# Attention values taken for two or three blocks of queries in one group of matmuls

## The chip, the cores and the metric

The kernel runs on one core of one Trainium2 chip. The metric is the device time of one execution in microseconds (us). The engines are named as in the profile: PE is TensorE's matmul, PEld its weight load, DVE is VectorE, ACT is ScalarE, POOL is GpSimd and SP is SyncE, which only issues transfers here.

## What is computed

There are 8 batches of 8 heads, 576 positions of 64 numbers each, in fp32. The attention weights are thresholded before they are normalised, and its output, with the heads side by side, goes through a feed-forward layer of 4608 tokens, 512 to 2048 to 512, with a squared ReLU.

```python
scores = scale * np.matmul(q, k.transpose(0, 1, 3, 2))
thresh = np.max(scores, axis=-1, keepdims=True) - tau
scores = np.where(scores >= thresh, scores, -1000000000.0)
scores = scores - np.max(scores, axis=-1, keepdims=True)
attn = np.exp(scores)
attn = attn / (np.sum(attn, axis=-1, keepdims=True) + 1e-09)
attn_out = np.matmul(attn, v)
x = attn_out.transpose(0, 2, 1, 3).reshape(B * S, H * D)
h = x @ w_in
r = np.maximum(h, 0.0)
out = (r * r) @ w_out
```

## The kernel before

The heads are taken in pairs, 32 pairs in all. The 576 queries of a pair are four blocks of 128 and one of 64 (NBLK is 4, REST is 64). A visit is a pair with a list of blocks, and a step is one block of one visit. Visits 0 to 3 take blocks 0 and 1 of the first four pairs, visits 4 to 7 take blocks 2, 3 and 4 of the same pairs, and from visit 8 on a visit takes all five blocks. So visits 0 to 3 are steps 0 to 7, visits 4 to 7 are steps 8 to 19, and visits 8, 9 and 10 are steps 20 to 34. Below, "v1 b1" is block 1 of visit 1.

One step goes through these stations:

- *Scores* (`scores`, L273, or L266 for the block of 64): PE multiplies the queries by the 576 keys, for both heads, into four of the eight PSUM banks. The next step's scores use the same four banks.
- *Maxima* (L310), exponents (L325 on ACT) and *threshold* (L337 on DVE): the threshold reads the scores a last time, and after it the banks are free for the next step's scores.
- *Division* (`divide`, L347 on POOL): the weights are normalised.
- *Turning*: for the values the weights are wanted with the keys on the partitions. Up to visit 10, PE turns them: `turn` transposes a block in three parts (L386; L393 and L399 for the block of 64), each into a PSUM bank, and ACT copies each part into `wT` (L387, L395, L400). This happens two steps after the block's own step. From visit 11 on (`by_dma`), DVE and transfers turn the weights instead.
- *Values* (`mix`, L502): PE multiplies the values v by the turned weights. One head gives 64 columns of output and the two heads stand side by side. For one block there are 10 fp32 matmuls (5 groups of keys, two heads), each of them two records in the trace. ACT then puts the result into `xT` (`put`, L485), the input of the feed-forward layer.

Two of the PSUM banks (4 and 5) serve the turns and the values in turn (`take("tx", (4, 5))`). A value group or a turn that gets a bank waits until ACT has copied out what stood there.

For visits 0 to 10 the values of a block are taken three steps after its own step. The table `mixes` says in which step which columns are taken, and the loop at the end of the kernel reads it. In such a step the order on PE is: scores of the step, first two parts of the turn of the block two steps back, perhaps a piece of the feed-forward layer, the values of the block three steps back, the third part of the turn, and further pieces.

A *piece* is a small part of the feed-forward layer for 256 tokens (a chunk). Pieces fill PE's time beside attention: `rate(s)` says how many us of pieces a step should take, a quarter of it is offered in four places of the step (`fill`), and a piece counts as PIECE_US, 1.76 us. Up to step `out_from` (34) the rate spreads the pieces of chunk 0 evenly over the steps that are left. A piece of the first product (L548) or the second (L730) of chunk 0 also waits until enough of the weights have been rounded. The rounding of the feed-forward weights is 32 parts, from step 2 to 33, one in most steps and two in steps 15, 18 and 22; one part takes two operations on ACT (L149, L150), two on DVE (L152, L154) and two on POOL (L156, L158). Chunk 0 is there from step 10, when the values of visit 3 have been taken. From step 35 on the pieces of chunk 1 follow.

All engines are scheduled by hand: each runs its instructions in the order in which the kernel emits them.

Of the kernel before, what the change touches and what calls it, by code (L numbers as in the profile page):

```python
# [19 lines left out]
def kernel(  # L20
# [10 lines left out]
    nc = tc.nc  # L31
    B, H, S, D = q.shape
    d_model, d_ff = moe_w_in.shape
    n_tokens = out.shape[0]
    P = 128
    HP = H // 2
    NPAIR = B * HP
    NBLK = S // P
    REST = S - NBLK * P
# [37 lines left out]
    wT = const.tile([P, S // REST + 1, NC9, REST], FP32, name="wT")  # L77
# [3 lines left out]
    at = RAW * 2 * WP  # L81
# [16 lines left out]
    g = const.tile([P, NFT, TCH], FP32, name="g")  # L98
# [104 lines left out]
    def arrived(t):  # L203
        assert all(x[0].tensor.name != t.tensor.name for x in loads)
# [149 lines left out]
    def take(what, among):  # L354
        used[what] += 1
        return bank[among[used[what] % len(among)]]
# [15 lines left out]
    def keep_bank(what):  # L372
# [2 lines left out]
        kept[what] = used["bank"]  # L375
        return to

    def turn(vis, i, part):

        w = weights[vis, i][0]  # L380
        ps = take("mm", (6, 7)) if early() and part == 1 else take("tx", (4, 5))
        ps = ps.rearrange("p (c n) -> p c n", n=P)
        if i < NBLK:
            for n in range(3):
                c = 3 * part + n
                nc.tensor.transpose(ps[:, n, :], w.rearrange("p u k -> p (u k)")[:, c * P:(c + 1) * P], ident)  # L386
            nc.scalar.copy(wT[:, 2 * i:2 * i + 2, 3 * part:3 * part + 3, :].rearrange("p g c q -> p c g q"),  # L387
                           ps[:, 0:3, :].rearrange("p c (g q) -> p c g q", g=2))
        elif part < 2:
            rows = slice(part * D, (part + 1) * D)  # L390
            for c in range(NBLK):
                at = part * REST + c * P
                nc.tensor.transpose(ps[:, c, 0:D], w[rows, 0, at:at + P], ident[rows, rows])  # L393
            at = part * (NBLK + 1)
            nc.scalar.copy(wT[:, 2 * NBLK, at:at + NBLK, :], ps[:, :, 0:D])  # L395
        else:

            for rows, keys in ((slice(0, D), slice(S - REST, S)), (slice(D, P), slice(0, REST))):
                nc.tensor.matmul(ps[rows, 0, 0:D], w[rows, 0, keys], ident[rows, rows], start=True, stop=True)  # L399
            nc.scalar.copy(wT[:, 2 * NBLK, NBLK, :], ps[:, 0, 0:D])  # L400

    blocks = {}
    outside = {}
# [66 lines left out]
    def put(n, first, ps, by_32s):  # L470

        b, pr = divmod(visits[n][0], HP)
        count = ps.shape[1]
        lo = (b * S + first) % RING
        assert b * S + first + count - RING <= read_to["x"]

        def to(x0, x1):
            at = (lo + x0) % RING
            return xT[:, pr, at:at + x1 - x0]

        fit = min(RING - lo, count)
        if not by_32s:
            for x0, x1 in ((0, fit), (fit, count)):
                if x0 < x1:
                    nc.scalar.copy(to(x0, x1), ps[:, x0:x1])  # L485
            return
        src = ps.rearrange("p (b u q) -> p b u q", u=2, b=4)
        if fit == count:
            nc.scalar.copy(to(0, count).rearrange("p (u b q) -> p b u q", u=2, b=4), src)
            return  # L490

        for u in range(2):
            b0 = min(max((fit - u * P) // 32, 0), 4)
            for x0, x1 in ((0, b0), (b0, 4)):
                if x0 < x1:
                    nc.scalar.copy(to(u * P + x0 * 32, u * P + x1 * 32).rearrange("p (b q) -> p b q", q=32),
                                   src[:, x0:x1, u, :])

    def mix(n, cols):

        def term(ps, u, c, at, rows=slice(0, P), first=False, last=False):
            nc.tensor.matmul(ps[u * D:(u + 1) * D, :], vs[n % 2][rows, u * (NBLK + 1) + c, :],  # L502
                             wT[rows, at // REST:(at + ps.shape[1]) // REST, NBLK if c == NBLK else u * (NBLK + 1) + c, :],
                             start=first, stop=last)

        above, below = slice(0, D), slice(D, P)
        arrived(vs[n % 2])
        if not by_dma(n):
            ps = take("tx", (4, 5))[:, 0:cols.stop - cols.start]
            for c in range(NBLK + 1):  # L510
                for u in range(2):
                    term(ps, u, c, cols.start, first=(c == 0), last=(c == NBLK))
            put(n, cols.start, ps, False)
            return
        n1, n2 = 2 * P + REST, 2 * P
        at = ODD if paired(n) and n % 2 else ONE
        one, two = bank[0], bank[4]
        groups = (one[:, 0:n1], at, (above, below)), (two[:, 0:n2], TWO, (below, above))
        for ps, x, _ in groups:
            for c in range(NBLK):  # L520
                for u in range(2):
                    term(ps, u, c, x, first=(c == 0))

        for ps, x, places in groups:
            for u, rows in enumerate(places):
                term(ps, u, NBLK, x, rows, last=True)
        put(n, 0, one[:, ONE - at:ONE - at + 2 * P], True)
        left = ODD if at == ODD else LEFT - at
        put(n, NBLK * P, one[:, left:left + REST], False)
        put(n, 2 * P, two[:, 0:n2], True)  # L530
# [281 lines left out]
    FIRST = TCH // P  # L812
# [3 lines left out]
    def paired(n):  # L816

        return n >= 3 * HP
# [7 lines left out]
    def by_dma(n):  # L826

        return n >= 3 * HP - 1
# [5 lines left out]
    mixes = {}  # L834
    complete = {}
    for s, (n, i) in enumerate(steps):

        if by_dma(n):
            mixed = {visits[n][1][-1]: (0, 3 if n % 2 else 4)}
        else:  # L840
            mixed = {x: (x, 3) for x in range(NBLK + 1)}
        if i in mixed:
            first, lag = mixed[i]
            cols = slice(first * P, S if by_dma(n) else min((i + 1) * P, S))
            mixes[s + lag] = (n, cols)
            g_ = visits[n][0]
            if g_ % HP == HP - 1:
                complete[s + lag] = g_ // HP * S + cols.stop
# [6 lines left out]
            j += 1  # L855
    PIECE_US = 1.76
    VALUES_US = 4.8
    SCORES_US = 1.25
    RESERVE = 3 * PIECE_US
    waiting = deque()  # L860
    state = {"us": 0.0, "left": 0.0, "step": 0, "free": False, "rounded": 0, "usable": 0, "then": [], "last": [], "made": 0}

    def early():
        return state["step"] < min(chunk_at)

    def pieces_of(j):

        todo = [((x // 4 + 1) * NMC, mlp_in, j, x) for x in range(NFT)]
        if j < PLAIN:
            todo += [(n_in + min(f + 1 + f // (NFT - 2), NFT), mlp_out, j, f) for f in range(NFT)]  # L870
        else:
            second = [(n_pieces, product, j, x, half) for x in range(len(PRODUCTS)) for half in range(2)]
            if j < SEVEN:
                return todo + second
            todo, rest = ([(n_pieces, unit, j, *x) for x in part] for part in UNITS)
            todo += second[0:2] + rest + second[2:]
        return todo
# [7 lines left out]
    def rate(s):  # L885


        if s < out_from:
            return PIECE_US * sum(x[2] == 0 for x in waiting) / (out_from - s)
        have = PIECE_US * len(waiting) - state["left"]  # L890
        best = 1e9
        at = s
        for e in sorted(chunk_at) + [END]:
            if e > s:
                have += sum(other(x) for x in range(at, e))
                at = e
                best = min(best, (have - (RESERVE if e < END else 0)) / (e - s))
                have += PIECE_US * sum(len(pieces_of(x)) for x in chunk_at.get(e, ()))
        return max(best, 0.0) - other(s)

    def other(s):

        us = sum(VALUES_US * (part if x >= first_late else x == s) for x, part in ((s, 0.75), (s + 1, 0.25))
                 if x in mixes and by_dma(mixes[x][0]))
        return us + (SCORES_US if s < NST else 0.0)

# [29 lines left out]
    for s, (n, i) in enumerate(steps):  # L936
        if s < HP * FIRST:
            x = int(n > 0 and i == 0)
        else:
            x = 2 if (n, i) in ((2 * HP - 2, FIRST + 1), (2 * HP - 1, FIRST + 1), (2 * HP, FIRST)) else 1  # L940
# [3 lines left out]
    out_from = next(s for s in range(NST) if sum(pieces[:s]) >= n_pieces)  # L944
# [10 lines left out]
    for s, (n, i) in enumerate(steps):  # L955
# [22 lines left out]
        if more:  # L978
            a, b, c, d = (s + 1, s + 5, s + 7, s + 8) if paired(n) else (s + 1, s + 2, s + 4, s + 4)
# [44 lines left out]
    def late_step(s):  # L1024
# [35 lines left out]
        if s == END:  # L1060
            values()
        quarter = rate(s) / 4 if s < END else 1e9
        made = state["made"]
        fill(quarter)
# [31 lines left out]
    for s in range(END + 1):  # L1096
# [9 lines left out]
        if on:  # L1106
            n, i = steps[s]
            at = visits[n][1].index(i)
            last = at == len(visits[n][1]) - 1
# [17 lines left out]
        if old:  # L1127
            turn(*old, 0)
            turn(*old, 1)
# [109 lines left out]
```

## Time and profile before

| what | us |
|---|---|
| median of 3 runs | 1335.18 |
| lowest and highest of them | 1333.57, 1335.20 |
| the profiled execution | 1333.83 |
| its span | 1332.0 |
| POOL busy from 100.6 to 120.5 us | 17.98 of 19.9 |
| PE busy from 156.0 to 210.4 us | 52.65 of 54.4 |
| values of visits 0 to 10 and later ones (L502), share of the chain that ended last | 10% |

The span is the time from the first to the last instruction on the core; the time of an execution is a little longer. The steps up to 34 end at about 210 us: step 4 starts its scores at 28.8 us, step 11 at 64.2, step 14 at 82.1, step 17 at 100.6, step 20 at 120.5, step 25 at 156.0 and step 35 at 210.4. In a line of the timeline the first two numbers are the start and how long it lasted, then come engine, line and operation, what was written and read, and in brackets how long the engine had been idle and what ended that. A group of L502 in that stretch is 20 records.

### The profile page before, as it was taken

Reading aid. Unit: us, or ns where it says so; the run is one execution under the profiler, and the core shown is the slowest. Engines: PE = TensorE matmul, PEld = TensorE weight load, DVE = VectorE, ACT = ScalarE, POOL = GpSimd, SP = SyncE. Lnnn points to the kernel's source line nnn. Section 1 sums busy time; section 2 is a strip of 40 time slices with the busy share of each in tenths; the row PEclk is TensorE's granted clock in tenths of the full one; section 3 lists DMA queues with packets and bytes.
Section 4 is the critical chain, followed back from the end, with each engine's and each line's share of the span. In section 5 each row is a group of like instructions: output and inputs, shape, how many; then the busy total and the mean of one; then the engine's idle time right before and its main releaser. Section 6 shows DMA issues by size and latency. Waiting matters only on the chain.

```text
span 1332.0 us, 25215 instructions
## 1 busy us (share of the span) xinstructions
PE 1295.4 (97%) x9112; PEld 1078.0 (81%) x9112; DVE 927.9 (70%) x2026; ACT 583.0 (44%) x1357; POOL 786.0 (59%) x915
## 2 busy tenths in 40 slices
PE   7898899999999999999999999999999999999998
PEld 5676556888787979797878878888897988889997
DVE  6877776877777878787777776868687877632131
ACT  4776674235262625343534343434443443421321
POOL 4689875775755565474665665747474747454351
PEclk7999999999999999999999999999999999999999
DMA  8764531648786968776766776676686767520000
GB/s 159 160 153 117 144 91 36 159 111 184 166 196 140 214 152 199 167 172 161 167 155 157 163 179 166 168 149 172 148 186 143 178 150 161 161 70 6 12 17 16
DMA packets 330126, 186.69 MB, mean 140 GB/s; under 512 B 291441, under 2 KB 291473, under 8 KB 323601
## 3 DMA queue, kind: packets, MB, share of 16 engines
q1 hardware_dynamic: 317696, 116.87, 46.5%
q0 software_dynamic: 10000, 67.92, 12.8%
q8 instruction: 72, 1.18, 0.4%
q10 hardware_dynamic: 2304, 0.29, 0.2%
q14 instruction: 54, 0.43, 0.1%
HBM read 109.22 MB, written 68.42 MB: 133 GB/s over the span
## 4 chain that ended last, share of the span: by engine, by line
PE 86%; DVE 4%; ACT 3%; POOL 2%; DMA 2%; issue 1%; SPq 0%; ACTq 0%; DVEq 0%; POOLq 0%
PE big L659 29%; PE big L765 28%; PE big L502 10%; PE big L289 8%; PE big L548 3%; PE big L273 3%; PE big L730 2%; PE big L386 2%; DVE st L310 1%; ACT wT L387 1%; DMA wT<-aside 1%; DVE w L337 1%; ACT w L325 1%; DMA aside<-turned 1%; POOL w L347 1%
## 5 line engine op out<-in xcount | busy, mean ns | idle before, releaser
L337 DVE SCALAR_TENSOR_TENSOR w<-big,st,w 128x576 f32<-128x576 f32 x269 | 207.1, 805 | 96.8 <-ACT w L325 96.5
L310 DVE TENSOR_REDUCE st<-big 128x1 f32<-128x576 f32 x288 | 204.2, 748 | 93.8 <-PE big L289 61.7
L347 POOL TENSOR_SCALAR w<-w,st 128x576 f32<-128x576 f32 x269 | 246.6, 926 | 26.4 <-DVE st L340 21.4
L765 PE MATMUL big<-wo,gsum 128*128 128x256 f32 x1088 | 243.8, 382 | 0.0
L765 PEld LDWEIGHTS big<-wo,gsum 128*128 128x128 f32 x1088 | 204.4, 190 | 37.0 <-issue 8.1
L659 PE MATMUL big<-xT,w_in_sb 128*128 128x128 f32 x1536 | 187.4, 277 | 1.3 <-DVE g L671 1.2
L659 PEld LDWEIGHTS big<-xT,w_in_sb 128*128 128x128 f32 x1536 | 178.5, 192 | 10.6 <-issue 8.1
L765 PE MATMUL big<-wo,g 128*128 128x256 f32 x816 | 185.3, 382 | 0.1
L325 ACT ACTIVATE w<-big,st 128x576 f32<-128x576 f32 x269 | 183.8, 734 | 0.0
L765 PEld LDWEIGHTS big<-wo,g 128*128 128x128 f32 x816 | 151.6, 190 | 26.1 <-issue 6.5
L502 PE MATMUL big<-wT,vs 128*64 128x128 f32 (+5 forms) x1700 | 164.2, 355 | 8.3 <-ACT wT L387 4.2
L502 PEld LDWEIGHTS big<-wT,vs 128*64 128x64 f32 (+1 forms) x1700 | 97.1, 137 | 72.0 <-issue 20.7
L322 ACT ACTIVATE st<-st 128x2 f32<-128x2 f32 (+1 forms) x148 | 30.3, 205 | 258.2 <-DVE st L310 257.1
L345 POOL TENSOR_SCALAR st<-st 128x2 f32<-128x2 f32 (+1 forms) x148 | 35.2, 238 | 169.3 <-DVE w L337 163.5
L408 POOL DMA_DIRECT2D aside<-turned x50 | 29.9, 597 | 177.9 <-DVE turned L437 173.7
L671 DVE TENSOR_TENSOR g<-big,g 128x512 f32<-128x512 f32 x96 | 64.7, 676 | 82.4 <-PE big L659 76.8
L289 PE MATMUL big<-kT,qT 64*128 64x256 f32 (+3 forms) x768 | 106.9, 416 | 0.0
L289 PEld LDWEIGHTS big<-kT,qT 64*128 64x128 f32 x768 | 84.5, 186 | 14.5 <-issue 5.0
L667 ACT ACTIVATE g<-g 128x512 f32<-128x512 f32 x96 | 60.2, 628 | 62.9 <-DVE g L671 62.7
L538 POOL TENSOR_TENSOR gsum<-g 128x512 f32<-128x512 f32 x34 | 46.2, 1358 | 69.8 <-ACT g L668 69.6
L668 ACT ACTIVATE g<-g 128x512 f32<-128x512 f32 x128 | 80.7, 630 | 4.1
L431 DVE STREAM_TRANSPOSE turned<-w 128x512 f32<-128x512 f32 x100 | 70.2, 702 | 0.0
(114 smaller groups left out, 2039.0 us busy)
## 6 DMA issues: line engine op xcount, KB each, us to landing
aside<-turned POOLq DMA_DIRECT2D x50, 1152.0 KB, 4.8
wT<-aside SPq DMA_DIRECT2D x200, 288.0 KB, 5.4
vs<-in_v_dram SPq DMA_DIRECT2D x72, 128.0 KB, 6.1
ql<-in_q_dram SPq DMA_DIRECT2D x126, 72.0 KB, 5.0
wo<-in_moe_w_in_dram SPq DMA_DIRECT2D x16, 512.0 KB, 4.6
wo<-in_moe_w_out_dram SPq DMA_DIRECT2D x16, 512.0 KB, 3.8
out_dram<-osb POOLq DMA_DIRECT2D x32, 256.0 KB, 3.6
kl<-in_k_dram SPq DMA_DIRECT2D x113, 72.0 KB, 2.9
```

The lines of the kernel that those rows point to most:

```text
L289: nc.tensor.matmul(big[to, at + x0:at + x1], lhsT, keys[u * D:(u + 1) * D, x0:x1], start=True, stop=True)
L310: nc.vector.tensor_reduce(out=mx[:, u:u + 1], in_=sc[u], axis=AX.XY, op=ALU.max)
L325: nc.scalar.activation(out=w[:, u, :].rearrange("p (h k) -> p h k", h=2), in_=sc[u], func=AF.Exp, bias=bias[:, u:u + 1], scale=SCALE)
L337: nc.vector.scalar_tensor_tensor(out=wu, in0=sc[u], scalar=thr[:, u:u + 1], in1=wu, op0=ALU.is_ge, op1=ALU.mult, accum_out=sm[:, u:u + 1])
L347: nc.gpsimd.tensor_scalar(out=w[:, u, :], in0=w[:, u, :], scalar1=z[:, u:u + 1], scalar2=rcp[:, u:u + 1], op0=ALU.add, op1=ALU.mult)
L431: move(wb[:, 0:h, :, :], whole_[:, 0, :, :, :])
L502: nc.tensor.matmul(ps[u * D:(u + 1) * D, :], vs[n % 2][rows, u * (NBLK + 1) + c, :], wT[rows, at // REST:(at + ps.shape[1]) // REST, NBLK ...
L659: nc.tensor.matmul(to[:, f, :], factor(j, p, q, c)[:, f * P:(f + 1) * P], part[:, c, :], start=(p in "125" and f == 0 and c == 0), stop=(p ...
L667: nc.scalar.activation(out=to, in_=to if src is None else src, func=AF.Relu)
L668: nc.scalar.activation(out=to, in_=to, func=AF.Square)
L671: nc.vector.tensor_tensor(out=x, in0=to, in1=x, op=ALU.add)
L765: nc.tensor.matmul(to, left[:, f, :], wo[:, slot, f, :], start=(f == 0), stop=(f == HF - 1))
```

## The change

The values of visits 0 to 10 are no longer taken block by block:

- visits 0 to 3: blocks 0 and 1 in one group of 256 columns, three steps after block 1;
- visits 4 to 7: blocks 2, 3 and 4 in one group of 320 columns, three steps after block 4;
- visits 8 to 10: blocks 0 and 1, blocks 2 and 3, and block 4, each three steps after its last block.

So a group stands in steps 4, 6, 8, 10, 13, 16, 19, 22, 24, 26, 27, 29, 31, 32, 34, 36 and 37, where there was one in every step from 3 to 37. As the turned weights of a visit must stay for longer, alternate visits of the first eight use alternate places in `wT` (`place_of`). The rate of pieces up to step 34 now also counts the values that are still to come, at 1.1 us per 128 columns (`early_values`), and takes off those of the step itself. Chunk 1 becomes available in step 22, where it was 21.

```diff
+    def place_of(n, i):
+
+        return n % 2 * 4 + 2 * i if n < HP else n % 2 * 5 + 2 * (i - FIRST) if n < 2 * HP else 2 * i
+
     def turn(vis, i, part):
 
         w = weights[vis, i][0]
+        to = place_of(vis, i)
...
-            nc.scalar.copy(wT[:, 2 * i:2 * i + 2, 3 * part:3 * part + 3, :].rearrange("p g c q -> p c g q"),
+            nc.scalar.copy(wT[:, to:to + 2, 3 * part:3 * part + 3, :].rearrange("p g c q -> p c g q"),
...
-            nc.scalar.copy(wT[:, 2 * NBLK, at:at + NBLK, :], ps[:, :, 0:D])
+            nc.scalar.copy(wT[:, to, at:at + NBLK, :], ps[:, :, 0:D])
...
-            nc.scalar.copy(wT[:, 2 * NBLK, NBLK, :], ps[:, 0, 0:D])
+            nc.scalar.copy(wT[:, to, NBLK, :], ps[:, 0, 0:D])
...
             ps = take("tx", (4, 5))[:, 0:cols.stop - cols.start]
+            at = place_of(n, cols.start // P) * REST
             for c in range(NBLK + 1):
                 for u in range(2):
-                    term(ps, u, c, cols.start, first=(c == 0), last=(c == NBLK))
+                    term(ps, u, c, at, first=(c == 0), last=(c == NBLK))
...
         else:
-            mixed = {x: (x, 3) for x in range(NBLK + 1)}
+            mixed = {1: (0, 3)} if n < HP else {NBLK: (FIRST, 3)} if n < 2 * HP else {1: (0, 3), 3: (2, 3), NBLK: (NBLK, 3)}
...
+    EARLY_VALUES_US = 1.1
...
         if s < out_from:
-            return PIECE_US * sum(x[2] == 0 for x in waiting) / (out_from - s)
+            return (PIECE_US * sum(x[2] == 0 for x in waiting) + sum(early_values(x) for x in range(s, out_from))) / (out_from - s) - early_values(s)
...
+    def early_values(s):
+
+        return EARLY_VALUES_US * (mixes[s][1].stop - mixes[s][1].start) / P if s in mixes else 0.0
```

## The prediction

> **What bounds the kernel now.** I read the page first: the busy shares, the row of slices and the chain that ended last.
>
> ```profile
> PE 1295.4 (97%) x9112; PEld 1078.0 (81%) x9112; DVE 927.9 (70%) x2026; ACT 583.0 (44%) x1357; POOL 786.0 (59%) x915
> ...
> PE   7898899999999999999999999999999999999998
> ...
> PE 86%; DVE 4%; ACT 3%; POOL 2%; DMA 2%; issue 1%; SPq 0%; ACTq 0%; DVEq 0%; POOLq 0%
> ```
>
> TensorE is the bound almost everywhere, but the change touches only steps 3 to 37, the first 245 us, and the only slices below 9 lie there. A slice is 33 us, so a step is smaller than one; I went on to TensorE's timeline of that stretch. Steps 3 and 4 (v1 b1, v2 b0), then 6 and 7:
>
> ```profile
> 21.55 3.02 PE L273 MATMUL big<-kT,qT 64*128 64x288 f32 x8 [1.71 <-DVE w L337]
> 24.50 1.54 PE L386 MATMUL big<-ident,wo 128*128 128x128 f32 x6
> 25.97 2.40 PE L502 MATMUL big<-wT,vs 128*64 128x128 f32 x20
> ...
> 28.81 1.56 PE L273 MATMUL big<-kT,qT 64*128 64x288 f32 x8
> ...
> 38.80 1.97 PE L273 MATMUL big<-kT,qT 64*128 64x288 f32 x8 [0.70 <-DVE w L337]
> 40.70 0.88 PE L386 MATMUL big<-ident,wo 128*128 128x128 f32 x6
> 41.50 1.31 PE L502 MATMUL big<-wT,vs 128*64 128x128 f32 x20
> 42.74 0.55 PE L386 MATMUL big<-ident,wo 128*128 128x128 f32 x3
> 43.99 1.97 PE L273 MATMUL big<-kT,qT 64*128 64x288 f32 x8 [0.70 <-DVE w L337]
> ```
>
> From step 5 to 9 every step takes 5.19 us and ends with TensorE waiting 0.70 us for VectorE's threshold (L337): the loop scores, turns, ACT copies, exponents, threshold is the bound, and the values (L502) lie beside it. Step 3's instructions take about twice as long. The windows of TensorE's clock say why (columns: window; its length; PE busy; clock; DMA share; GB/s):
>
> ```profile
> 7.91:11.33 3.42, 2.31 (x16) 1.00 0.72 128
> 11.33:14.74 3.41, 0.04 (x1) 1.00 0.80 188
> ...
> 18.15:21.57 3.42, 1.71 (x9) 0.50 0.79 112
> 21.57:24.98 3.41, 3.41 (x10) 0.50 0.67 107
> 24.98:28.39 3.41, 3.41 (x26) 0.50 0.78 131
> 28.39:31.80 3.41, 3.41 (x29) 1.00 0.82 215
> ```
>
> The clock is at half from 14.74 to 28.39, four windows of 3.41 us. A window filled with scores (64 of 128 rows) didn't release it; the window with step 3's turns and values did. In the middle stretch, steps 14 to 24, weights are rounded on POOL (busy 17.98 of 19.9 us from 100.6 to 120.5), and the chain of waits runs through both engines:
>
> ```profile
> 103.15 1.28 POOL w_in_sb L158
> ...
> 104.48 0.70 PE big L548 x2
> 105.18 1.24 PE big L502 x20
> 106.42 0.48 PE big L386 x3
> 106.90 1.73 PE big L548 x8
> ```
>
> A piece of the first product waits for its weights; behind it in TensorE's queue the values, a turn and a second piece stand before step 18's scores. From 156 to 210 us TensorE is busy 52.65 of 54.4, and from 218 us without a break.
>
> [...] a group takes 1.24 us at 128 columns and 0.73 at 64 (199.41 in the chain), so 0.51 per 64 columns and 0.22 fixed.
>
> **The change part by part.** *Size of a group*: by that line 256 columns cost 0.22+4x0.51=2.26 us, 320 cost 2.77. Two blocks save 2x1.24-2.26=0.22, three save 2x1.24+0.73-2.77=0.44. Over visits 0 to 3 (0.22 each), 4 to 7 (0.44) and 8 to 10 (2x0.22) TensorE does 4.0 us less. What counts is where.
>
> *Steps 2 to 10.* Without step 3's values (2.33 us at half clock) the scores of step 4 wait for VectorE, whose first head ends at 28.27: they start at 28.40 instead of 28.81. But the window 24.98 to 28.39 then holds turns until about 26.5 and nothing more, like the window at 18.15 that kept half clock. The next holds scores and a little turning, like 21.57: half. The release comes only with step 4's new 256 columns, in 31.80 to 35.21. At half clock: scores 2.95 from 28.40, turns 1.47, so values from 32.82; they need 4.5, do 2.4 until 35.21, and the rest in 1.05 at full clock; with the last turn (0.48) step 5's scores start at 36.8, not 33.60: **+3.2 us**. Then steps without values keep 5.19 (VectorE's loop; TensorE's idle grows from 0.7 to 1.9), and steps 6 and 8 need 2.70 up to the values, 2.26 and 0.48, 5.44: +0.25 each. Step 10: values from 61.95, plus 2.26 and 0.48, 64.7 against 64.23: +0.5. Together **+4.2**.
>
> *Planner.* early_values adds the values still to come to the rate and takes the step's own off: about 3.4 us of pieces in a step without values (before 2.45 everywhere), 0.6 beside 320 columns, 1.2 beside 256. Worked through, steps 11, 12, 14, 15, 17, 18, 20, 21 have two pieces and 13, 16, 19 none; steps 11 to 24 have 19 pieces where they had 20. Where no piece stands before the last turn, the turn takes over the values' wait for a PSUM bank (0.24, or 0.40 after a fifth block).
>
> *Steps 11 to 16.* Before 17.87 and 18.54 us. After, step 11: 2.3 to the last turn, 0.38, two pieces 3.55, so 6.2; 12: 5.8; 13: 2.05+2.77+0.43=5.3; together 17.3 (**-0.5**). Steps 14 to 16: 6.2; 6.34 (unchanged: VectorE's threshold releases the next scores, not TensorE); 5.3: 17.9 (**-0.65**).
>
> *Steps 17 to 24.* In 17 and 20 values lay on the chain behind POOL; they go. POOL's rounding of step 15 starts 1.4 earlier, as step 14's scores-to-scores time shrank, so step 17's piece gets its weights at 103.0 and step 18's scores start at 103.0+0.63+0.45+1.83=106.0, not 108.56. Step 18 keeps its VectorE chain; 19 with 320 columns takes 5.3 (5.04 before). From step 17 to 20: **-1.1**. Step 20 again loses 1.24 and some wait for weights: **-1.4**. Steps 21 and 22 (320 columns and a double rounding): +0.1 and +0.25. Step 23 loses 1.24 less 0.2 of waiting: -1.05. Step 24: the wait of 1.57 for ACT is covered by a piece that comes first, and one piece is left over for later: -1.35. Together **-4.55**.
>
> *Steps 25 to 37.* Summed the same way, with the piece left over (1.75): **+0.75**; the last two groups of visit 10: -0.2. From step 38 on the instructions are the same.
>
> *Places and wait-free changes.* place_of only changes addresses of wT; visits alternate so that a late group isn't overwritten. Cost nothing. The copy of 320 columns on ACT (0.18 to about 0.44) stands behind the exponents; priced above at 0.25 in step 22. Chunk 1 comes a step later, but its first piece runs in step 35: nothing.
>
> Sum: +4.2-0.5-0.65-4.55+0.75-0.2 = **-0.95 us** on the profiled execution (1333.83 us, span 1332.0), 1332.9. The median shown, 1335.18, is 1.35 above that execution; the times stand in two pairs (1333.6 to 1333.8, 1335.2), and a release of the clock a window later would cost about that much. The changed kernel's dense stretch in step 4 is 6.5 us long, so it should catch a whole window wherever the windows fall. I put it between 1332.9 and 1334.2, at **1333.5**.
>
> Unknown costs: the half clock's share, from 0 (released on time) to +5 more; a window of about 40% work at full clock in steps 5, 7, 9 has no row here except 7.91 (2.31 of 3.41, kept full); I take that it stays full. The gains of steps 17 to 24, from -1.7 (TensorE's saving alone) to -6.
>
> **The rivals.** *A, faster*: the clock is released as early as before, or the middle stretch gives all its slack: 3 less, 1330. For: gaps of 0.4 to 1.6 us in front of values and scores there. Against: the windows above. 0.20. *B, slower*: the half clock outlasts step 4, or comes back in a step without values. Place: steps 4 to 9. It decides if the activity asked for is above what turns and values gave in the window at 24.98, or if a 40% window counts as idle. Price: rest of step 4 +1.1, step 5 at 6.85 instead of 5.19, the first half of step 6 +2.2: 5 more, **1339**. For: two full-looking windows did not release it. Against: the window at 7.91 kept it. 0.15. *C*: the middle stretch stays bound by POOL and gives only TensorE's own saving; +4.2-1.15-1.7+0.75-0.2=+1.9 on the profiled execution, 1335.7 to 1337.1, so 1336.5. For: POOL busy 90%. Against: the chain, which has values in it at 105.18. 0.20. That a group doesn't cost what the line gives (2.77) is small: 0.3 us each.
>
> **How the numbers follow.** Forecast 0.45. Measured differences below 0.2% (2.7 us) I take for no change: 1332.5 to 1337.9. The forecast lies inside it, with 0.12 of its 0.45 below; A is faster (with 0.18 of 0.20); C leaves 0.05 above; B slower. Faster 0.30, same 0.50, slower 0.20. The range holds A's centre and B's: 1329.5 to 1339.
>
> **What would show it.** Right: half clock until about 35 us; step 5's scores near 36.8; groups of 2.3 and 2.8 us; step 18's scores about 2 us closer to step 11's; the same order from step 38 on. Wrong: full clock at 28.4, half clock again after 36, or POOL waiting in steps 16 to 21 where it now has none.

## The result, and the profile after

| what | before | after |
|---|---|---|
| median of 12 runs each, us | 1334.16 | 1337.95 |
| lowest and highest, us | 1333.57, 1335.88 | 1336.04, 1339.78 |
| the profiled execution, us | 1333.83 | 1336.04 |
| its span, us | 1332.0 | 1334.2 |
| mean granted clock of TensorE | 0.994 | 0.986 |

The ratio after to before is 1.0025, with a 95% interval from 1.0016 to 1.0034: the changed kernel is slower by about 3.8 us. The profiled execution of after is the shortest of its twelve, so the difference of the two profiles (2.2 us) understates the change.

The page of after, in the parts that the prediction showed of before (busy time; 40 slices; the chain that ended last):

```profile
PE 1296.4 (97%) x8752; PEld 1067.3 (80%) x8752; DVE 933.5 (70%) x2026; ACT 582.2 (44%) x1339; POOL 785.0 (59%) x915
...
PE   6799999999999999999999999999999999999998
...
PE 87%; DVE 5%; DMA 3%; ACT 2%; issue 1%; POOL 1%; SPq 1%; ACTq 0%; DVEq 0%; POOLq 0%
```

TensorE has 360 matmul records fewer (8752 for 9112; there are as many columns of values, in wider groups) and is busy 1.0 us *longer*, where the prediction had 4.0 us less. That fits matmuls that run more slowly, and the granted clock says the same: 0.986 for 0.994. The first two slices have lost a tenth each, and slices four and five, from 100 to 167 us, have gained one. So the loss lies near the start and a gain behind it.

The starts of the steps' scores, from the two timelines, show how much of it lies where:

```
                      before    after   difference since the line above
step 5 begins          33.6      35.4    +1.8
step 11 begins         64.2      73.0    +7.0
steps 11 to 13         17.87     17.33   -0.5
steps 14 to 16         18.54     18.5     0.0
steps 17 to 19         19.8      18.3    -1.5
steps 20 to 24         35.5      30.5    -5.0
steps 25 to 34         54.4      55.8    +1.4
steps 35 to 37         31.1      30.8    -0.3
step 38 begins        241.6     244.3    +2.8 in all
```

Up to step 11 the change loses 8.8 us, 1.8 of them before step 5. From there to step 38 it wins 6.0. From step 38 on the instructions are the same.

TensorE's timeline of after, steps 4 to 7 (start, length, engine, line; in brackets the idle time before it and what ended that):

```profile
31.96 3.03 PE L507 MATMUL big<-wT,vs 128*64 128x256 f32 x20
34.92 0.55 PE L391 MATMUL big<-ident,w 128*128 128x128 f32 x3
35.40 1.25 PE L273 MATMUL big<-kT,qT 64*128 64x288 f32 x8
36.58 1.20 PE L391 MATMUL big<-ident,w 128*128 128x128 f32 x9
40.20 3.02 PE L273 MATMUL big<-kT,qT 64*128 64x288 f32 x8 [2.42 <-DVE w L337]
43.16 1.54 PE L391 MATMUL big<-ident,wo 128*128 128x128 f32 x6
44.63 3.52 PE L507 MATMUL big<-wT,vs 128*64 128x256 f32 x20
48.08 0.55 PE L391 MATMUL big<-ident,wo 128*128 128x128 f32 x3
```

Step 5 has no values: its scores and turns end at 37.78, and TensorE then waits 2.42 us for the threshold. Step 6 starts after 4.8 us, no later than a step did before (5.19), but its scores take 3.02 us, where step 6 of the kernel before took 1.97 after a wait of the same kind, and its values 3.52. The windows of TensorE's clock in the same stretch (window; its length; PE busy and records; clock; DMA share; GB/s):

```profile
33.32:36.74 3.42, 3.42 (x28) 1.00 0.59 94
36.74:40.15 3.41, 1.04 (x9) 1.00 0.95 217
40.15:43.56 3.41, 3.36 (x10) 0.50 0.76 129
43.56:46.98 3.42, 3.42 (x18) 0.50 0.75 126
46.98:50.39 3.41, 3.41 (x29) 1.00 0.60 179
50.39:53.80 3.41, 0.99 (x7) 1.00 0.14 30
53.80:57.22 3.42, 3.42 (x12) 0.50 0.62 99
```

Read the third and fourth columns together, one row after the other. The window in which step 5 waits is busy for 1.04 of 3.41 us, and the next one has half the clock. Two windows later the clock is back. Then step 7 waits, 0.99 us busy, and it falls again. DMA isn't what the two weak windows have in common (0.95 and 0.14). In this execution the clock was at half from 12.84 to 19.67, 23.08 to 33.32, 40.15 to 46.98, 53.80 to 60.63 and 67.46 to 70.87: ten windows after the first release, where before had four.

The middle stretch did what the change does. The chain of waits of after around steps 17 and 18 (start, length, what):

```profile
110.96 1.28 POOL w_in_sb L158
112.24 0.04 issue
112.28 0.70 PE big L554 x2
112.98 0.33 PE big L391 x3
113.31 1.73 PE big L554 x8
115.04 1.22 PE big L273 x8
```

Before, 1.24 us of values (L502) stood between the first piece and the turn. They are gone from step 17, and the chain is shorter by them. The groups themselves, from the timeline of steps 16 and 24:

```profile
105.52 2.91 PE L507 MATMUL big<-wT,vs 128*64 128x320 f32 x20 [0.24 <-ACT wT L392]
...
154.91 2.38 PE L507 MATMUL big<-wT,vs 128*64 128x256 f32 x20
```

Counted from the start of the group to that of the next operation they take 2.84 and 2.31 us.

### The profile page after: what moved, and what is told of

Read it like the earlier page. It is cut to its first block, busy times and chain, and to the rows that moved or that the text cites. A ratio compares the mean times of both kernels' runs of the same rounds, so it can differ in the third digit from the quotient of the medians.

```text
span 1334.2 us, 24472 instructions
## 1 busy us (share of the span) xinstructions
PE 1296.4 (97%) x8752; PEld 1067.3 (80%) x8752; DVE 933.5 (70%) x2026; ACT 582.2 (44%) x1339; POOL 785.0 (59%) x915
## 4 chain that ended last, share of the span: by engine, by line
PE 87%; DVE 5%; DMA 3%; ACT 2%; issue 1%; POOL 1%; SPq 1%; ACTq 0%; DVEq 0%; POOLq 0%
PE big L665 28%; PE big L771 27%; PE big L507 11%; PE big L289 8%; PE big L554 4%; PE big L273 3%; PE big L391 2%; PE big L736 2%; DMA wT<-aside 1%; DVE st L310 1%; DMA aside<-turned 1%; DVE w L337 1%; ACT w L325 1%; PE big L266 1%; ACT wT L392 0%
## 5 line engine op out<-in xcount | busy, mean ns | idle before, releaser
L507 PE MATMUL big<-wT,vs 128*64 128x256 f32 (+4 forms) x1340 | 162.1, 408 | 4.1 <-DMA wT<-aside 2.0
L507 PEld LDWEIGHTS big<-wT,vs 128*64 128x64 f32 (+1 forms) x1340 | 84.0, 139 | 74.3 <-issue 20.6
L677 DVE TENSOR_TENSOR g<-big,g 128x512 f32<-128x512 f32 x96 | 64.7, 676 | 82.5 <-PE big L665 76.9
```

Source lines behind the costliest of these rows:

```text
L677: nc.vector.tensor_tensor(out=x, in0=to, in1=x, op=ALU.add)
```

## The experiments

The theory: the loss of the first 73 us is not in the groups of two blocks but in the steps that lost their values. Their windows hold so little work that the clock falls, and the step behind pays. The rivals: the groups or the new places themselves cost it; the late release of the clock in step 4 is all of it; the pieces, dealt out differently, cost it. The starts of the steps already speak against the second (1.8 of the 8.8 us are lost before step 5), and the third can't hold before step 10, since there are no pieces until then. Each ratio below is to the kernel before, run on the same chip (medians 1334.61, 1334.05 and 1334.28 beside e1 to e4, e5 to e8 and e9 to e11). Times in steps are from the profiled executions.

### e1: visits 0 to 3 block by block again

```diff
-            mixed = {1: (0, 3)} if n < HP else ...
+            mixed = {x: (x, 3) for x in range(NBLK + 1)} if n < HP else ...
```

> The changed kernel, with visits 0 to 3 taken block by block again (one group of 128 columns in every step from 3 to 10), all else as changed. Clock theory (the loss is all in steps 3 to 10, where steps without values let TensorE's clock fall to half; the groups of visits 4 to 10 gain about 5.7 us): half clock only from about 14.7 to 28.4, step 11's scores near 64.3 instead of 73.0, step 35's about 140.5 later as in the changed kernel, time 1328 to 1330 us. Rival (the longer groups hold up the next scores wherever they stand, clock or no clock): step 11 near 64 too, but no gain behind it, 1334 to 1336.

Measured: 1334.91 us (1332.20 to 1336.77, 12 runs), ratio 0.9998 [0.9990, 1.0007]. A miss of 5 us, and by the time the rival is right; e5 below decides between the two. The part that the run was aimed at came as expected: step 11 starts at 64.3, as before, and the clock is at half from 14.41 to 28.06 and then full until 113.40. The loss is behind that. The windows of e1, in a place where the clock fell in neither kernel:

```profile
106.57:109.98 3.41, 3.01 (x27) 1.00 0.45 154
109.98:113.40 3.42, 0.93 (x5) 1.00 0.01 2
113.40:116.81 3.41, 2.68 (x7) 0.50 0.85 286
```

And e1's timeline there, from the last piece of step 18 to the values of step 19:

```profile
108.92 1.99 PE L554 MATMUL big<-xT,w_in_sb 128*128 128x256 f32 x8
114.13 2.26 PE L266 MATMUL big<-kT,qmid 128*128 128x288 f32 x4 [3.22 <-ACT turned L150]
116.18 1.49 PE L391 MATMUL big<-ident,w 128*128 128x128 f32 x6
117.60 4.19 PE L507 MATMUL big<-wT,vs 128*64 128x320 f32 x20
```

The budget of pieces that the planner carries from step to step (`state["left"]`) is +0.47 us at step 11 in e1 and was -0.32 in after, since the early steps took off other values. That moves one piece from step 18 to step 17. Step 18 has no values and now only one piece; TensorE waits 3.22 us before step 19's scores, and the clock falls. The same thing as in steps 5, 7 and 9, at another place: steps 17 to 19 take 23.3 us where after takes 18.3.

### e2: groups in visits 0 to 3 alone

```diff
-            mixed = {1: (0, 3)} if n < HP else {NBLK: (FIRST, 3)} if ...
+            mixed = {1: (0, 3)} if n < HP else {x: (x, 3) for x in range(NBLK + 1)}
```

> Only visits 0 to 3 in groups of two blocks, visits 4 to 10 block by block as before. Clock theory: the clock goes up and down as in the changed kernel, step 11's scores near 73, and nothing is won behind it: 1342 to 1344 us. Rival: the groups of visits 4 to 10 are part of the loss, so this is nearer to the kernel before, 1335 to 1338.

Measured: 1340.99 (1339.99 to 1342.38), ratio 1.0048 [1.0033, 1.0063]. Step 11 starts at 75.0, later than in after, and steps 11 to 34 take 143.7 us (after 140.5, before 146.1). The loss stands with these visits, but this run can't say whether it is the groups or the emptied steps.

### e3: work put back into steps 3, 5, 7 and 9

After, with one group of 128 columns in each of these steps, of the first block's values, whose result nobody reads. This is more work than after does.

```diff
+            if keep:
                 put(n, cols.start, ps, False)
...
+        if s in (3, 5, 7, 9):
+            mix(steps[s - 3][0], slice(0, P), False)
```

> The changed kernel, and in steps 3, 5, 7 and 9 a group of 128 columns more, the first block's values, whose result nobody reads: work added (4 x 1.24 us of TensorE), nothing taken away. Clock theory: the clock is released near 28.4 and stays full, step 11's scores come at about 65.3 (the 256-column groups cost 0.25 to 0.5 in four steps), 1329 to 1331 us, faster than the changed kernel by some 7. Rival (steps 3 to 10 lose by the length of the groups, or by TensorE's work): no faster than the changed kernel, 1337 to 1341.

Measured: 1329.54 (1328.64 to 1331.11), ratio 0.9963 [0.9950, 0.9976]: 80 matmul records *added* make the kernel 8.4 us faster than after, by the medians. The clock is full from 27.18 on, step 11 starts at 64.7, and steps 11 to 34 take 140.5 as in after. The windows of e3 at steps 5 and 6:

```profile
34.01:37.42 3.41, 3.41 (x35) 1.00 0.74 114
37.42:40.83 3.41, 2.71 (x18) 1.00 0.92 239
40.83:44.25 3.42, 3.42 (x29) 1.00 0.84 110
```

The middle window holds the same wait, shorter by the unread values, and keeps the clock full; its DMA share is as high as in the window of after that lost it. With the groups of two blocks, the new places and the new dealing of pieces all in it, the early stretch costs what it cost before, within 0.5 us. So it is the emptied steps.

### e4: the rate of pieces blind to the values

```diff
-    EARLY_VALUES_US = 1.1
+    EARLY_VALUES_US = 0.0
```

> The changed kernel with the values counted at 0 us in the rate, so that pieces are spread evenly again and may stand beside a group of 320 columns. Clock theory: steps 3 to 10 unchanged (step 11's scores near 73), and the order of pieces behind is worth less than 1.5 us: 1336.5 to 1339.5. Rival (the gain of 5.7 us behind step 11 is the planner's): step 11 to step 35 take 143 or more instead of 140.5, 1340 or more.

Measured: 1347.74 (1347.06 to 1349.13), ratio 1.0097 [1.0080, 1.0113]; steps 11 to 34 take 150.5 us, so it went the way of the rival. With pieces dealt out evenly, steps 15 and 18 have neither values nor a second piece, and TensorE waits for the threshold before the next step's scores. The timeline of e4, steps 16 and 19:

```profile
106.64 1.21 PE L266 MATMUL big<-kT,qmid 128*128 128x288 f32 x4 [3.06 <-DVE w L337]
...
128.13 2.15 PE L266 MATMUL big<-kT,qmid 128*128 128x288 f32 x4 [3.05 <-DVE w L337]
```

After either wait the clock is at half for one window (107.76 to 111.18 and 128.24 to 131.66). Two windows of 3.41 us at half can account for at most 3.4 of the 10.0 us that e4 takes longer than after in steps 11 to 34; how the rest is shared between the waits and the pieces that stand beside long groups was not taken apart. The change's own correction of the rate, which fills the steps without values with pieces, is what keeps the middle stretch clear of this. There are no pieces before step 10, so it can't help the first ten steps.

### e5: e1 with the budget of after

```diff
+        if s == 11:
+            state["left"] = -0.32
```

> As e1 (visits 0 to 3 block by block, the rest as in the changed kernel), with the planner's leftover at step 11 set to the -0.32 us that it has in the changed kernel; in e1 it is +0.47, which moves one piece from step 18 to 17 and leaves TensorE idle for 3.2 us in step 18, where the clock fell. Clock theory: with the changed kernel's pieces no window is that empty, half clock only until about 28, 1327 to 1330 us. Rival (e1 shows that the groups of visits 4 to 10 win nothing): 1334 to 1336.

Measured: 1328.12 (1327.31 to 1328.94), ratio 0.9957 [0.9942, 0.9971], as expected. Half clock only from 16.23 to 26.47; step 11 at 63.8; steps 11 to 34 in 140.0. e5 and after differ in the groups of visits 0 to 3 alone: 9.8 us between the medians, 9.2 of them before step 11.

### e6: the kernel before with less work

In steps 3, 5, 7 and 9 the values take one of the five groups of keys: four times 16 records less. This leaves out part of those values.

```diff
-            for c in range(NBLK + 1):
+            parts = 1 if state["step"] in (3, 5, 7, 9) else NBLK + 1
+            for c in range(parts):
```

> The kernel before, where the value groups of steps 3, 5, 7 and 9 take one of the five groups of keys and leave the other four out: 64 records less in all, no group longer, no turned weights moved. Clock theory: each of these steps has a window under a third of work, the clock falls as in the changed kernel, step 11's scores come 5 to 8 us later than before, 1338 to 1343 us although work is left out. Rival (the loss comes from the longer groups or from the places): no slower than before, 1333 to 1334.6.

Measured: 1337.04 (1336.32 to 1337.43), ratio 1.0020 [1.0010, 1.0030], a little less than expected, as only 4.7 us are lost by step 11. No group, no place and no rate of pieces is changed here; work is taken out of four steps, and the kernel is 3.0 us slower. The timeline of e6, step 5 and the start of step 6:

```profile
37.58 0.44 PE L502 MATMUL big<-wT,vs 128*64 128x128 f32 x4
37.95 0.55 PE L386 MATMUL big<-ident,w 128*128 128x128 f32 x3
40.07 3.02 PE L273 MATMUL big<-kT,qT 64*128 64x288 f32 x8 [1.57 <-DVE w L337]
```

and its windows:

```profile
36.78:40.19 3.41, 1.84 (x15) 1.00 0.93 235
40.19:43.60 3.41, 3.41 (x11) 0.50 0.62 100
```

A window more than half busy, by this view, lost the clock after a wait of 1.57 us. The section on the hardware comes back to that.

### e7: work added to step 2

e5, with eight unread transposes on TensorE at the end of step 2, where it waits for the threshold at half clock.

```diff
+        if s == 2:
+            to = take("tx", (4, 5))
+            for x in range(8):
+                nc.tensor.transpose(to[:, x % 4 * P:x % 4 * P + P], ident, ident)
```

> As e5, with eight transposes of the identity into a free bank at the end of step 2, where TensorE waits 1.7 us for VectorE at half clock; nobody reads them. Clock theory: the window that holds step 2's turns is then full, the clock is released near 21.5 instead of 28, steps 3 and 4 lose 1.5 to 2.5 us, 1325.5 to 1328 us. Rival (the first release hangs on something else than the work in a window, or these steps are VectorE's anyway): equal to e5 within 0.5.

Measured: 1326.81 (1326.36 to 1327.43), ratio 0.9946 [0.9929, 0.9962]: the fastest of all, 7.2 us below before beside it and 11 below after. Its timeline, step 2 and the scores of step 3, and its windows:

```profile
18.95 2.18 PE L391 MATMUL big<-ident,w 128*128 128x128 f32 x9
20.92 1.70 PE L1171 MATMUL big<-ident 128*128 128x128 f32 x8
22.83 1.97 PE L273 MATMUL big<-kT,qT 64*128 64x288 f32 x8 [0.21 <-DVE w L337]
```

```profile
15.44:18.85 3.41, 2.86 (x8) 0.50 1.12 306
18.85:22.27 3.42, 3.42 (x17) 0.50 0.77 118
22.27:25.68 3.41, 3.20 (x19) 1.00 0.64 102
```

The added transposes (L1171) fill the wait: only 0.21 us of it is left. The window they stand in releases the clock two windows after it had fallen, so step 3 already runs at full speed: from its scores to those of step 4 it takes 5.20 us, where e5 takes 6.85 (21.09 to 27.94). How much of that reaches the end is less clear. By the medians e7 is 1.3 us faster than e5, but these are four executions each, and the ranges and intervals overlap. In the profiled executions both start step 11 at the same time (63.85 and 63.78), as in e7 the clock was first released later (12.03 for 5.99), and the 1.0 us between them arises after step 38, where the instructions are the same.

### e8 and e9: which groups bring the gain

e8 is e5 with the blocks of visits 8 to 10 taken singly; e9 is after with every block taken singly, so that only the places and the rate remain.

```diff
e8
+            mixed = {NBLK: (FIRST, 3)} if HP <= n < 2 * HP else {x: (x, 3) for x in range(NBLK + 1)}
e9
+            mixed = {x: (x, 3) for x in range(NBLK + 1)}
```

> As e5, with visits 8 to 10 block by block too, so that only visits 4 to 7 are taken in groups of three. If the middle stretch (values off the chain behind POOL) carries the gain, this keeps most of it: 1328.5 to 1331 us, up to 2 slower than e5. Rival (the gain is TensorE's fixed cost per group, shared by all visits): half of the gain lost, 1331 to 1333.

> The changed kernel with every visit taken block by block: of the change only the places in wT and the planner's count of values are left, so the values stand where they stood before and only pieces move (step 15 one as before, 17 and 20 two in a row). If the places are free and the planner alone is worth little: 1332.5 to 1335.5 us, clock as before. Rival (part of what the changed kernel wins behind step 11 is the order of pieces, not the groups): 1330 to 1332.

Measured: e8 1331.78 (1329.57 to 1334.16, 16 runs), ratio 0.9981 [0.9974, 0.9989], in the rival's range; e9 1333.51 (1332.58 to 1335.83, 12 runs), ratio 0.9997 [0.9988, 1.0005], as expected. Steps 11 to 34 take 146.1 us before, 144.8 in e9, 143.2 in e8 (its fastest execution) and 140.0 in e5. Places and rate alone make no difference to the whole time that can be told from none. In these steps, though, the profiled e9 is 1.3 us shorter than before, and e2, which has no group of visits 4 to 10 either, 2.4, so part of the gain may be the order of pieces. The groups of visits 8 to 10 gain 3.7 us by the medians (e8 against e5, intervals apart). For those of visits 4 to 7 it is 1.7 us (e9 against e8); there the intervals just touch, and e8 has the budget of pieces of e5, which e9 has not. Both seem to gain, but the second share is not sharp.

### e10: larger groups in visits 8 to 10

e7 with blocks 0 to 2 and blocks 3 and 4 in a group each.

```diff
+            ... else {2: (0, 3), NBLK: (3, 3)}
```

> As e7, with visits 8 to 10 in two groups (blocks 0 to 2, blocks 3 and 4) instead of three. By the fixed cost of a group (0.22 us) three groups fewer save 0.7 us: 1326 to 1327. Rival (clock): step 34 then has neither values nor a piece, and if its window falls to a third of work or less, the clock falls there: 1328 to 1330.

Measured: 1328.69 (1327.73 to 1330.68), ratio 0.9959 [0.9944, 0.9974]: 1.9 us above e7 by the medians, though the intervals overlap; the gain that was expected did not come. The clock is not the cause (mean 0.997). The timeline of e10, step 35:

```profile
203.15 1.24 PE L273 MATMUL big<-kT,qT 64*128 64x288 f32 x8 [1.63 <-DVE wo L337]
...
208.56 3.45 PE L507 MATMUL big<-wT,vs 128*64 128x384 f32 x20
```

The first group of visit 10 has moved from step 34, where TensorE waits 1.63 us for the threshold at the end anyway, into step 35, where it is the bound: step 35 takes 15.8 us where it takes 12.2 in e7. The saving of a larger group (one fixed cost) is smaller than what its place costs.

### e11: less unread work than e3

e3 with the unread groups of steps 5, 7 and 9 on three of the five groups of keys.

```diff
+            mix(steps[s - 3][0], slice(0, P), 5 if s == 3 else 3)
```

> As e3, but the unread groups in steps 5, 7 and 9 take three of the five groups of keys (0.65 us of streaming instead of 1.09), so that the emptiest windows of these steps hold about 0.35 to 0.44 of work, where windows of 0.33 fell and of 0.42 stayed so far. Clock theory with a bound in between: some executions fall once or more, others not, so times spread over 1330 to 1336 us, between e3 (1329.5) and the changed kernel (1338). Rival (any work in each step is enough): as e3, 1329 to 1330.5, no spread.

Measured: 1329.52, ratio 0.9970 [0.9957, 0.9983]; three executions at 1329.1 to 1329.5 and two at 1332.1 and 1332.2. In the profiled one the clock never fell after 29.34. Counted as in the section on the hardware, its emptiest windows in steps 5, 7 and 9 held 0.47 to 0.52, more than the 0.35 to 0.44 expected, so it says nothing of where the clock falls. With the windows laid otherwise over the same timeline the emptiest would hold 0.33. The two slower executions fit that, with a mean clock of 0.990 where the others have 0.992 to 0.995, but they have no timeline: inconclusive.

## Why the prediction was wrong

The prediction was 1333.5 us, with no change as the likeliest; measured were 1337.95, inside the range and slower by more than can be told from none. Rival B happened, the half clock that "comes back in a step without values", and its price was 1339. It had a chance of 0.15. One of the prediction's own signs of being wrong came with it: half clock again after 36.

The step that failed stands among the unknown costs: "a window of about 40% work at full clock in steps 5, 7, 9 has no row here except 7.91 (2.31 of 3.41, kept full); I take that it stays full." The windows of steps 5 and 7 did not stay full; they lost the clock at 40.15 and 53.80, and it fell again at 67.46. Two things were wrong in reading the row at 7.91. It was busy for 68% of its length, so it says nothing of 40%. And 40% is the mean over a step of 5.2 us: the clock changed on a grid of 3.41 us, and one such window can hold nearly the whole wait, as 36.74 to 40.15 does with 1.04 us of work.

What followed from it, by the prediction's own terms:

- *Half clock until about 35 us in step 4*: right, but for one window at full clock from 19.67, which wasn't forecast. Released at 33.32, by the window with step 4's 256 columns (29.91 to 33.32); step 5's scores at 35.4, forecast 36.8.
- *Steps 5 to 10*: the failed term. 31.6 us were forecast from step 5's scores to step 11's (36.8 to 64.2+4.2) and 37.6 measured. Three falls to half clock cost 6.0. B had said 5, but for one longer stay at half in steps 4 to 6, so that the two figures are close is luck. With that, +4.2 became +8.8. That it is the emptied steps is shown from both sides: filled again (e3), the loss is gone; emptied in the kernel before (e6), it appears.
- *Size of a group*: 2.26 and 2.77 forecast, 2.31 and 2.84 measured. Right, and so is the fixed cost of about 0.2 (0.53 more for 64 columns more leaves 0.19 of the 2.31); what its cause is, no run here shows.
- *Steps 11 to 16*: -0.5 forecast for the first three and -0.5 measured; -0.65 for the next three and 0.0 measured (18.5 us for the forecast 17.9). Why is open.
- *Steps 17 to 24*: -4.55 forecast. Measured -1.5 and -5.0, together -6.5: just beyond the bound of -6. Most of what was missing lies in steps 20 to 24, where the parts add to -3.45.
- *Steps 25 to 34*: +0.75 forecast, +1.4 measured. *Steps 35 to 37*: -0.2 and -0.3.
- *Places cost nothing*: shown by e9 together with the rate (0.9997).

From step 11 to 34 the sum was -4.95, and -5.7 was measured. The direction held; that the sums are so close is partly luck, as misses of +0.65, -1.95 and +0.65 cancel. Rival C, which gave the middle stretch only TensorE's own saving, fell by the same figure. Rival A's early release did not last in after: the clock came back at 19.67 and was lost again at 23.08. e7 shows an early release that lasts, by work at the end of step 2.

One thing the prediction credited to the change as a detail turned out to hold the rest up: the rate that fills steps without values with pieces. Without it (e4) steps 11 to 34 take 10 us more, a third of it at most by the clock itself, and one piece in a different step (e1) costs 6.8 (e1 against e5, by the medians).

The version that comes out of this is e7: groups in visits 4 to 10 only, the pieces as in after, and step 2 filled. It is 0.54% faster than before; e5, without the filled step 2, is 0.43% faster, and the two can't be told apart with certainty.

## What to carry to other kernels

Where an engine's clock falls after stretches with little work, as TensorE's did here (busy for 1.04 of 3.41 us from 36.74 of after, then at 0.50), idle time on it isn't free cover: before work is taken from a step in which TensorE waits, cut the stretch into windows as long as the clock's own (3.413 us in these profiles), wherever they may begin, and count what the emptiest would hold, not the step's mean. Savings belong in steps where the engine is the bound; in the others, work that nobody needs can be worth more than none (8.4 us in e3). And a planner that deals out filler should see the holes that a change makes, since one piece in the wrong step can cost as much as the change gains (6.8 us in e1).

## What the runs showed of the hardware

The clock changed in steps of 3.413 us in every profile. The offset of that grid to the kernel's start differs from one profiled execution to the next (the first release comes between 6.0 and 8.2 us in ten of them, 6.02 in after and 7.93 in before, and between 12.0 and 12.3 in three, 12.03 in e7), so the same wait can fall into one window or be split over two. That fits the wide spread of e1 (1332 to 1337) and e8 (1329.6 to 1334.2), though no run sets the offset.

Busy time as the windows show it doesn't sort the windows: 1.84 of 3.41 us lost the clock in e6, while 1.52 (the scores from 9.40 to 10.92) kept it in e5. Something else does. For the following table each matmul record of a window was counted by the time its columns take to stream, times the share that its form has of 128\*128, the largest in the timelines; scores of 64\*128 count half. The time is 0.241 us for 288 columns at full clock (the L266 records from 85.00 of after start 0.242 apart), in proportion for other widths, and twice that at half: transposes of 128 columns start 0.109 apart at full clock (from 36.75 of after) and 0.213 at half (from 23.89).

```
window from          counted share   then
full clock
 before   11.35           0.01       falls
 after    36.74           0.25       falls
 after    50.39           0.16       falls
 e1      109.98           0.22       falls
 e4      104.35           0.30       falls
 after     9.43           0.33       falls
 e6       36.78           0.36       falls
 e5        9.40           0.36       stays
 e3       37.42           0.42       stays
 e8       36.70           0.43       stays
 before    7.93           0.56       stays
half clock
 before   14.76           0.65       stays half
 before   21.59           0.69       stays half
 e2       42.36           0.75       stays half
 e5       23.06           0.78       released
 e3       23.77           0.79       released
 after    16.26           0.81       released
 before   25.00           0.90       released
 e7       18.85           0.96       released
```

Counted so, the windows part: those that lost the clock hold 0.36 or less (e6 at 36.78), those that kept it 0.36 or more (e5 at 9.40); those that stayed at half hold up to 0.75 (e2 at 42.36), those that were released 0.78 or more (e5 at 23.06). The same count over all whole windows of the thirteen profiles up to 1300 us finds nothing against it: 30 falls, none above 0.36, and no window that stayed full below 0.36; 56 windows that stayed half, up to 0.75, and 43 releases, from 0.78. Without the weight for the form they don't part: the window of before at 21.59 streams for 0.90 of its time, mostly scores, and stays half, while e3's at 23.77 with 0.89 is released. These are the windows nearest to the bounds and a few clear ones; the windows of before begin 0.02 us later than in the prediction, on the grid of the recorded clock changes. It is a fit to these thirteen profiles and the author's estimate, and the bounds hang on where in its record a matmul is taken to stream (here from the start; counted back from the record's end, 0.38 and 0.41 part the windows at full clock, while at half two are released at 0.73 and one stays at 0.75).

The length of the wait alone sorts less well: 1.57 us before step 6 of e6 lost the clock, and 1.63 us before step 35 of e10, across the edge of two windows (202.33), did not (its clock was full from 21.43 on).

A window did not have to be empty to lose the clock: windows that did a quarter to a third of their possible work lost it (0.25 at 36.74 of after, 0.33 at 9.43). And transposes against an identity matrix counted as work: in after's window at 16.26 they make 0.56 of the 0.81, and e7's window at 18.85 holds little else, counts 0.96 and released the clock.
